# Block-causal attention with a SwiGLU layer: the seven products of the last 1,024 tokens in two PSUM tiles of one bank, where they stood in one tile of two banks

## The chip, the core and the metric

The kernel runs on one core of one Trainium2 chip. The metric is device time in microseconds (us) of one execution; of several executions the median is given. The core has a matmul engine (TensorE, PE in the profile, with PEld for its weight loads), VectorE (DVE), ScalarE (ACT), GpSimd (POOL) and SyncE (SP), which here mostly issues DMAs. Each engine runs its own instructions in program order; between engines they wait on semaphores.

## The reference, cut to what matters

```python
def _attn_ref(q, k, v):                       # each [8, 8, 576, 64]: batch, head, token, channel
    scores = (1.0 / np.sqrt(64)) * np.matmul(q, k.transpose(0, 1, 3, 2))
    scores = np.where(mask, scores, -1e9)     # a query sees the blocks of 64 tokens up to its own
    attn = softmax(scores)
    return np.matmul(attn, v)

x = attn_out.transpose(0, 2, 1, 3).reshape(4608, 512)
g, val = x @ w_gate, x @ w_val                # 512 x 1536 each
return (g * sigmoid(g) * val) @ w_out         # 1536 x 512
```

All is 32-bit floating point. The kernel keeps every operand as a high and a low part and computes a product as three matmuls: high x high, high x low, low x high.

## The kernel before, in words

**Tasks and planner.** `tile_block_causal_attention_swiglu_kernel` runs nothing at first. It records tasks with `add` (line 154): an engine, a cost, a rank, a function that emits the instructions, the tasks it follows, and the buffers (`Buf`, line 134) that it uses. A DMA is recorded by `dma` (line 182) as a task of SP, with `moves`, the time that its bytes take. When all tasks stand, the planner `in_order` (line 1637) plays them through with its own costs (`act_us`, `dve_us`, `mm_us`): on each engine it takes the task of lowest rank whose predecessors are done and whose buffers have a free place, and of a DMA it takes its data to be there at `queue + 0.9`. What it returns is the order in which all is emitted, so its costs set the order of the instructions on each engine and no time on the chip. `keep_busy` (line 1732) puts small filler matmuls (L1741) into gaps that the planner sees on TensorE. The waits between engines come from the tile framework as the instructions are emitted: an instruction that reads or writes a tile waits for those before it that wrote or read the same tile.

**PSUM.** Three pools (lines 310 to 312) fill the eight banks: `at`, two places of two banks ([128, 2, 512] floats); `gv`, two places of one bank; `po`, one place of two banks. The attention uses `at`.

**The first 3,584 tokens** go in 14 tiles of XT = 256 tokens through `feed_forward`. A step makes two chunks of 128 of the 1,536 hidden channels: gate products (L1114 to L1116) into one `gv`, value products into the other, then tanh on ScalarE (L1147) and on VectorE L1150 (which reads the gate's `gv` and frees it) and L1155 (which reads the value's), the split in a high part (L1160, ScalarE) and a low part (L1163, VectorE), and output products (L1205 to L1207) that add up in `po`. `leave` (line 1225) copies finished sums out of PSUM (L1235) and stores them.

**The last 1,024 tokens** go in two pairs (PAIRS = 2) of 512 tokens. `bring_pair` (line 1293) loads the attention's result (L1326, `x_d`) and the inverse sums (`r_load`, L1335, four DMAs from `r_d`), multiplies the two (`divide`, L1341, 1.2 us on VectorE), makes sums of its parts (L1345 to L1347) and splits them into high and low parts (L1361, L1364). This work stands between the steps of the tiles before it. `feed_pair` (line 1373) then makes 12 steps per pair (NFC = 12), each for 128 hidden channels of the gate and of the value layer. It uses a scheme of seven products for a 2 x 2 block product (Strassen's, in Winograd's form), where the sums of weights come from `sum_d` by a load of 2 x 512 KB per step (L1396) and the weights of the output layer from `wo_d` (L1528, 512 KB). In the text the seven products are four groups of matmuls of 256 columns, all on line L1424:

- **P1** (task `u1`): A11 x B11 and A12 x B21, 12 matmuls, into bank 1 of an `at` tile
- **P2** (`u2`): S3 x T3 and S1 x T1, 12 matmuls, into bank 0 of the same tile
- **P3** (`u3`): S2 x T2, 6 matmuls, added to the first half of bank 1
- **P4** (`u4`): A22 x T4 and S4 x B22, 12 matmuls, added to bank 0

Between them the banks are read: ScalarE copies half of P1's bank to SBUF (L1463, task `a1`) and VectorE adds the other half (L1472, `d1`). The same is done for P2's (L1466 `a2`, L1475 `d2`) and, behind P3, L1469 (`a3`) and L1478 (`d3`, no PSUM). L1482 (`d4`) reads the whole of bank 0 behind P4. P3 writes over what `a1` read, so it follows `d1`; P4 follows `d2`. Then come tanh (L1502), the two multiplies (L1505, L1510) and the split (L1515 on ScalarE, L1518 on VectorE) that gives the operand of the **output products** (L1546 to L1548): 12 matmuls of 512 columns per step. They run two steps later: a step's own go to `chain["late"]`, then to `chain["down"]`, and hang on the `u2` of the step after next. They add up over the 12 steps of a pair in four accumulators, two `gv` tiles and the two banks of `po`. Two `at` tiles take turns from step to step.

```python
        accs = [Buf("gv") for _ in range(2)]
        accs += [Buf("po")] * 2
...
            ps, c, t, hh = Buf("at"), Buf("mx", "c"), Buf("t"), Buf("hhl")
...
            u3 = work([product("S2", T2, 1, 0, False, True)], [u2, d1], u2)
            u4 = work([product("A22", T4, 0, 1, False, True), product("S4", B22, 0, 0, False, True)], [u3, d2], u3)
```

Of the kernel before, what the change touches and what calls it, by code (L numbers as in the profile page):

```python
# [12 lines left out]
ALU = mybir.AluOpType  # L13
# [5 lines left out]
def kernel(  # L19
# [17 lines left out]
    nc = tc.nc  # L37
# [10 lines left out]
    NFC = DFF // P  # L48
    SCALE = 1.0 / (D**0.5)
    XT = 256  # L50
# [93 lines left out]
    class Task:  # L144
        def __init__(self, engine, cost, rank, fn, after, bufs, port, mode):
            self.engine, self.cost, self.rank, self.fn = engine, cost, rank, fn
            self.bufs, self.waits, self.next, self.ready = bufs, 0, [], 0.0
            self.moves, self.port, self.mode = 0.0, port, mode

            self.prev = None  # L150

# [17 lines left out]
    def act_us(n, psum=False, more=0.0):  # L169
        return (0.05 if psum else 0.093) + n * 0.000833 + more  # L170
# [1122 lines left out]
    def bring_pair(n, t0):  # L1293
# [26 lines left out]
        for j in range(K):  # L1320
# [30 lines left out]
            l = dma(R, 5e5, load, [*l, turn], [xs], 2, packet=2048)  # L1351
            m = dma(R, 5e5, r_load, [*inv, turn], [rs], 4, packet=2048)
            if n and not j:
                held.extend((n, x) for x in (l, m))
# [18 lines left out]
    def feed_pair(n, t0, xs):  # L1373
# [5 lines left out]
        last_pair = n == PAIRS - 1  # L1379
        accs = [Buf("gv") for _ in range(2)]  # L1380
        accs += [Buf("po")] * 2

        def sums(m):
            return accs[m][0] if m < 2 else accs[m][0][:, m - 2]

# [3 lines left out]
        for i in range(NFC):  # L1389
# [17 lines left out]
            soon, chain["soon"] = chain["soon"], chain["up"]  # L1407
            ps, c, t, hh = Buf("at"), Buf("mx", "c"), Buf("t"), Buf("hhl")

# [7 lines left out]
            def product(a, o, bank, half, begin, end):  # L1417
                def emit(ps=ps, stationary=stationary):
                    to = ps[0][:, bank, half * XT : (half + 1) * XT]
                    for j in range(K):  # L1420
# [13 lines left out]

            def work(products, after, prev):
                def emit(products=products):
# [16 lines left out]

            B11, B21, B22, T1, T2, T3, T4 = range(7)
            u1 = work(
                [product("A11", B11, 1, 0, True, False), product("A12", B21, 1, 1, False, True)],
                [sl, chain["up"]],
                None,
            )
            u2 = work([product("S3", T3, 0, 1, True, False), product("S1", T1, 0, 0, False, False)], [u1], u1)  # L1460

            def copies(c=c, ps=ps):
                nc.scalar.copy(c[0][:, 0], ps[0][:, 1, 0:XT])  # L1463

            def copies3(c=c, ps=ps):
                nc.scalar.copy(c[0][:, 3], ps[0][:, 0, XT : 2 * XT])  # L1466

            def copy_u(t=t, ps=ps):
                nc.scalar.copy(t[0][:, 0:XT], ps[0][:, 1, 0:XT])  # L1469

            def c11(c=c, ps=ps):
                nc.vector.tensor_tensor(c[0][:, 0], ps[0][:, 1, XT : 2 * XT], c[0][:, 0], ALU.add)  # L1472

            def v57(c=c, ps=ps):
                nc.vector.tensor_tensor(c[0][:, 3], ps[0][:, 0, 0:XT], c[0][:, 3], ALU.add)  # L1475
# [4 lines left out]
            def c12(c=c, t=t, ps=ps):  # L1480
                u = t[0][:, 0:XT].rearrange("p (a n) -> p a n", a=1).to_broadcast([P, 2, XT])
                nc.vector.tensor_tensor(  # L1482
                    c[0][:, 1:3], ps[0][:, 0].rearrange("p (a n) -> p a n", a=2), u, ALU.add
                )

            a1 = add("ACT", act_us(XT, True), E, copies, [u1], [ps, c])
            d1 = add("DVE", dve_us(XT), E, c11, [a1], [ps, c])
            a2 = add("ACT", act_us(XT, True), E, copies3, [u2], [ps, c])
            d2 = add("DVE", dve_us(XT), E, v57, [a2], [ps, c])
            u3 = work([product("S2", T2, 1, 0, False, True)], [u2, d1], u2)  # L1490
            u4 = work([product("A22", T4, 0, 1, False, True), product("S4", B22, 0, 0, False, True)], [u3, d2], u3)
            chain["up"] = u4
            in_place[at] = [u4]
            a3 = add("ACT", act_us(XT, True), E, copy_u, [u3], [ps, t])
            d3 = add("DVE", dve_us(XT), E, c22, [a3, d2], [c, t], True)
            d4 = add("DVE", dve_us(w), E, c12, [a3, u4], [ps, c, t])

            def gate():
                return c[0][:, 0:2].rearrange("p a n -> p (a n)")

# [18 lines left out]

            a = add("ACT", act_us(w), E, tanh, [d1, d3, d4], [c, t])  # L1520
            a = add("DVE", dve_us(w), E, silu2, [a], [c, t], True)
            a = add("DVE", dve_us(w), E, gated, [a], [c, t], True)
            a = add("ACT", act_us(w), E, high, [a], [t, hh])
            a = add("DVE", dve_us(w), E, low, [a], [t, hh], True)

# [10 lines left out]
            for x in chain["down"]:  # L1536
                u2.next.append(x)
                x.waits += 1
# [98 lines left out]
    def in_order():  # L1637
# [42 lines left out]
        while events:  # L1680
# [3 lines left out]
            for e in engines:  # L1684
# [28 lines left out]
                if t.moves:  # L1713
                    queue = max(queue, end + 0.65) + t.moves
                    done = queue + 0.9
                heapq.heappush(events, done)
# [64 lines left out]
```

## Time and profile before

| | |
|---|---|
| runs | 1208.89, 1207.72, 1207.88 us: median 1207.88 |
| the profiled execution's own time | 1205.76 us |
| its span in the profile | 1203.7 us (about 2 us of the time lie outside) |
| mean granted clock of TensorE | 0.993 of full speed |
| busy: PE, DVE, ACT, POOL | 96%, 74%, 55%, 27% of the span |
| the chain that ended last, by engine | PE 81%, DMA 6%, ACT 6%, DVE 5%, SP's queue and issue 1% each |
| DMA | 222.60 MB, 185 GB/s over the span |

Busy time is the time in which an engine has an instruction under way. For TensorE the ends of matmuls are modelled, so distances from start to start are the surer reading: 12 matmuls of a group that follow each other show it. The "idle before" of a row is the time in which the engine had nothing under way ahead of that instruction, and the name behind it is the instruction whose semaphore came last. The granted clock is TensorE's share of full speed (2.4 GHz); 0.50 is the lower of its two levels (1.2 GHz).

### The profile page before, as it was taken

The page shows a single profiled execution, that of the slowest core. Times are in us where ns is not written, and L with a number is a line of the kernel's source. Part 1 is how long each engine was busy: PE and PEld are TensorE (multiplying, and loading weights), DVE is VectorE, ACT ScalarE, POOL GpSimd, SP SyncE. Part 2 cuts the span into 40 slices and gives each one's busy share as a digit, 9 for nine tenths or more (in the row PEclk, how much of TensorE's full clock was granted, in tenths as well). Part 3 has the DMA queues.
Part 4 walks back from the last instruction along what each step waited for, and adds up shares of the span by engine and source line. Part 5 has one row for each costly group of instructions (what it writes and reads, how often), then busy time and mean ns, then how long its engine had stood idle before and what let it go on. Part 6 is the DMA issues. An engine that isn't in the chain of part 4 may idle for free.

```text
span 1203.7 us, 22411 instructions
## 1 busy us (share of the span) xinstructions
PE 1158.4 (96%) x8560; PEld 1032.3 (86%) x8560; DVE 890.5 (74%) x1506; ACT 662.3 (55%) x1222; POOL 326.2 (27%) x139
## 2 busy tenths in 40 slices
PE   8999999999999999999999999999999899889897
PEld 6678778888899989899989989998989888878886
DVE  6989988676788889897988988898974525544443
ACT  6888866637565756654647457577552313322222
POOL 3122100144543253343233334344353000000000
PEclk9999999999999999999999999999999999999999
DMA  8658756766566566766666757665653748555550
GB/s 221 183 147 222 209 175 234 193 184 167 156 163 214 146 191 182 220 180 189 192 192 196 200 164 207 189 198 151 181 163 127 236 148 285 197 201 193 188 180 35
DMA packets 281066, 222.60 MB, mean 185 GB/s; under 512 B 196032, under 2 KB 228048, under 8 KB 280960
## 3 DMA queue, kind: packets, MB, share of 16 engines
q1 hardware_dynamic: 278384, 220.46, 61.7%
q8 instruction: 67, 1.10, 0.4%
q10 hardware_dynamic: 2576, 0.72, 0.3%
q14 instruction: 39, 0.32, 0.1%
HBM read 184.16 MB, written 36.96 MB: 184 GB/s over the span
## 4 chain that ended last, share of the span: by engine, by line
PE 81%; DMA 6%; ACT 6%; DVE 5%; issue 1%; SPq 1%; POOL 0%; DVEq 0%; ACTq 0%; POOLq 0%
PE gv L1114 12%; PE gv L1116 11%; PE gv L1115 11%; PE at L1424 9%; PE at L792 7%; PE po L1205 6%; PE po L1207 6%; PE po L1206 5%; PE at L579 5%; DMA wo<-in_moe_w_out_dram 2%; DMA wo<-r_d 1%; ACT ob L974 1%; DMA wo<-wo_d 1%; PE gv L1546 1%; PE gv L1548 1%
## 5 line engine op out<-in xcount | busy, mean ns | idle before, releaser
L843 POOL PARTITION_ALL_REDUCE mx<-mx x48 | 179.2, 3780 | 242.2 <-DVE mx L720 173.2
L724 POOL PARTITION_ALL_REDUCE mx<-mx x80 | 144.5, 1855 | 353.9 <-DVE mx L720 147.3
L1114 PE MATMUL gv<-xhl,v_all 128*128 128x256 f32 x672 | 190.1, 283 | 1.1 <-DVE t L1150 1.1
L1116 PE MATMUL gv<-xhl,v_all 128*128 128x256 f32 x672 | 187.1, 278 | 0.0
L1115 PE MATMUL gv<-xhl,v_all 128*128 128x256 f32 x672 | 186.9, 278 | 0.0
L748 DVE TENSOR_TENSOR sc<-sc,mx 128x640 f32<-128x640 f32 (+6 forms) x168 | 125.4, 781 | 10.4 <-POOL mx L724 10.4
L1114 PEld LDWEIGHTS gv<-xhl,v_all 128*128 128x128 f32 x672 | 126.4, 188 | 6.0 <-issue 2.5
L752 ACT ACTIVATE sc<-sc 128x1024 f32<-128x1024 f32 (+3 forms) x104 | 106.0, 1031 | 38.7 <-DVE sc L748 38.0
L1115 PEld LDWEIGHTS gv<-xhl,v_all 128*128 128x128 f32 x672 | 126.6, 188 | 0.7
L1116 PEld LDWEIGHTS gv<-xhl,v_all 128*128 128x128 f32 x672 | 126.3, 188 | 0.1
L1205 PE MATMUL po<-wo,hhl 128*128 128x512 f32 x300 | 119.3, 398 | 0.9 <-DMA wo<-wo_d 0.9
L1207 PE MATMUL po<-wo,hhl 128*128 128x512 f32 x300 | 117.3, 391 | 0.2 <-DVE hhl L1163 0.2
L1206 PE MATMUL po<-wo,hhl 128*128 128x512 f32 x300 | 117.5, 392 | 0.0
L720 DVE TENSOR_TENSOR mx<-mx,sc 128x128 f32<-128x128 f32 (+2 forms) x180 | 103.9, 579 | 2.4 <-ACT sc L484 0.5
L1114 PE MATMUL gv<-xhl,g_even 128*128 128x256 f32 x336 | 97.5, 290 | 3.9 <-DVE t L1150 3.9
L1160 ACT CAST hhl<-t 128x512 fp32r<-128x512 f32 x84 | 52.1, 620 | 79.4 <-DVE t L1155 68.8
L1116 PE MATMUL gv<-xhl,g_even 128*128 128x256 f32 x336 | 95.6, 284 | 0.0
L1115 PE MATMUL gv<-xhl,g_even 128*128 128x256 f32 x336 | 95.6, 284 | 0.0
L1114 PE MATMUL gv<-xhl,g_odd 128*128 128x256 f32 x336 | 95.3, 284 | 0.0
L1163 DVE TENSOR_TENSOR hhl<-t,hhl 128x512 fp32r<-128x512 f32 x84 | 74.2, 884 | 27.2 <-ACT hhl L1160 26.5
L1116 PE MATMUL gv<-xhl,g_odd 128*128 128x256 f32 x336 | 93.8, 279 | 0.0
L1115 PE MATMUL gv<-xhl,g_odd 128*128 128x256 f32 x336 | 93.8, 279 | 0.0
(246 smaller groups left out, 2820.3 us busy)
## 6 DMA issues: line engine op xcount, KB each, us to landing
wo<-wo_d SPq DMA_DIRECT2D x176, 512.0 KB
v_all<-sum_d SPq DMA_DIRECT2D x48, 512.0 KB
sum_d<-wo SPq DMA_DIRECT2D x48, 256.0 KB
v<-in_v_dram SPq DMA_DIRECT2D x64, 128.0 KB
out_dram<-ob SPq DMA_DIRECT2D x32, 256.0 KB
qk<-in_q_dram SPq DMA_DIRECT2D x112, 72.0 KB
qk<-in_k_dram SPq DMA_DIRECT2D x104, 72.0 KB
x_d<-xu SPq DMA_DIRECT2D x24, 288.0 KB
```

What stands on the lines that cost most here:

```text
L720: nc.vector.tensor_tensor(into, prev, of(c), op)
L724: nc.gpsimd.partition_all_reduce(m, m, channels=P, reduce_op=bass_isa.ReduceOp.max)
L748: nc.vector.tensor_tensor(piece(c), scores_of(c), m, ALU.subtract)
L752: nc.scalar.activation(x, x, AF.Exp)
L843: nc.gpsimd.partition_all_reduce(m, m, channels=P, reduce_op=bass_isa.ReduceOp.add)
L1114: nc.tensor.matmul(o, lhsT=hi[:, d], rhs=xhi[:, 0:w], start=first, stop=False)
L1115: nc.tensor.matmul(o, lhsT=hi[:, d], rhs=xlo[:, 0:w], start=False, stop=False)
L1116: nc.tensor.matmul(o, lhsT=lo[:, d], rhs=xhi[:, 0:w], start=False, stop=last)
L1205: nc.tensor.matmul(po, lhsT=hi, rhs=whi, start=i + y == 0, stop=False)
L1206: nc.tensor.matmul(po, lhsT=hi, rhs=wlo, start=False, stop=False)
L1207: nc.tensor.matmul(po, lhsT=lo, rhs=whi, start=False, stop=i + y == NFC - 1)
L1424: nc.tensor.matmul(to, lhsT=s, rhs=m, start=begin and j == 0 and s is hi and m is xhi, stop=j == K - 1 and s is lo, skip_group_check=True,)
```

## The change

In `feed_pair` the `at` tile `ps` becomes two `gv` tiles, `ab` for P1 and P3 and `cd` for P2 and P4; both are taken anew in each step, and there are two `gv` places in all, so each step uses the same two banks. The output sums stand in `po` (the first two) and in one `at` tile (the other two). The functions between get new names and one that nothing called goes. Besides, the planner counts 0.08 to 0.11 us more for the ScalarE and VectorE tasks of `feed_pair` and 3 us more until the inverse sums of a pair are there (`m.more`), and in the last step of the last pair the output products that wait hang on `u4` instead of `u2`. What is computed is the same. Lines behind line 1350 move by +1, those behind the removed function by -2.

```diff
-            self.prev = None
+            self.prev, self.more = None, 0.0
...
             m = dma(R, 5e5, r_load, [*inv, turn], [rs], 4, packet=2048)
+            m.more = 3.0
...
-        accs = [Buf("gv") for _ in range(2)]
-        accs += [Buf("po")] * 2
+        accs = [u for u in (Buf("po"), Buf("at")) for _ in range(2)]
 
         def sums(m):
-            return accs[m][0] if m < 2 else accs[m][0][:, m - 2]
+            return accs[m][0][:, m % 2]
...
-            ps, c, t, hh = Buf("at"), Buf("mx", "c"), Buf("t"), Buf("hhl")
+            ab, cd, c, t, hh = Buf("gv"), Buf("gv"), Buf("mx", "c"), Buf("t"), Buf("hhl")
...
-                def emit(ps=ps, stationary=stationary):
-                    to = ps[0][:, bank, half * XT : (half + 1) * XT]
+                def emit(ps=(cd, ab)[bank], stationary=stationary):
+                    to = ps[0][:, half * XT : (half + 1) * XT]
...
-            def copies(c=c, ps=ps):
-                nc.scalar.copy(c[0][:, 0], ps[0][:, 1, 0:XT])
...
+            def copy_1(c=c, ab=ab):
+                nc.scalar.copy(c[0][:, 0], ab[0][:, 0:XT])
...
-            a1 = add("ACT", act_us(XT, True), E, copies, [u1], [ps, c])
-            d1 = add("DVE", dve_us(XT), E, c11, [a1], [ps, c])
-            a2 = add("ACT", act_us(XT, True), E, copies3, [u2], [ps, c])
-            d2 = add("DVE", dve_us(XT), E, v57, [a2], [ps, c])
-            u3 = work([product("S2", T2, 1, 0, False, True)], [u2, d1], u2)
-            u4 = work([product("A22", T4, 0, 1, False, True), product("S4", B22, 0, 0, False, True)], [u3, d2], u3)
+            a1 = add("ACT", 0.11 + act_us(XT, True), E, copy_1, [u1], [ab, c])
+            d1 = add("DVE", 0.08 + dve_us(XT), E, c11, [a1], [ab, c])
+            a2 = add("ACT", 0.11 + act_us(XT, True), E, copy_7, [u2], [cd, c])
+            d2 = add("DVE", 0.08 + dve_us(XT), E, add_5, [a2], [cd, c])
+            u3 = work(ab, [product("S2", T2, 1, 0, False, True)], [u2, d1], u2)
+            u4 = work(cd, [product("A22", T4, 0, 1, False, True), product("S4", B22, 0, 0, False, True)], [u3, d2], u3)
...
-            a3 = add("ACT", act_us(XT, True), E, copy_u, [u3], [ps, t])
-            d3 = add("DVE", dve_us(XT), E, c22, [a3, d2], [c, t], True)
-            d4 = add("DVE", dve_us(w), E, c12, [a3, u4], [ps, c, t])
+            a3 = add("ACT", 0.11 + act_us(XT, True), E, copy_16, [u3], [ab, t])
+            d3 = add("DVE", 0.08 + dve_us(XT), E, c22, [a3, d2], [c, t], True)
+            d4 = add("DVE", 0.08 + dve_us(w), E, c12, [a3, u4], [cd, c, t])
...
             for x in chain["down"]:
-                u2.next.append(x)
+                (u4 if last_pair and i == NFC - 1 else u2).next.append(x)
                 x.waits += 1
...
                 if t.moves:
                     queue = max(queue, end + 0.65) + t.moves
-                    done = queue + 0.9
+                    done = queue + 0.9 + t.more
```

The engines' orders are the same up to about 940 us; behind that they differ, because the planner's costs and buffers do. Three places show how.

First piece: ScalarE in one step of the last 1,024 tokens before, with what each instruction waits for (`PE_49` is a count of TensorE's, `DVE_49` of VectorE's, `Activation_49` of ScalarE's own).

```order
L1463 COPY mx_0_10285<-at_0_185 128x256 [waits PE_49]
L1466 COPY mx_0_10285<-at_0_185 128x256 [waits DVE_49,PE_49]
L1515 CAST hhl_0_115<-t_0_117 128x512 [waits DVE_49]
L1469 COPY t_0_953<-at_0_185 128x256 [waits DVE_49]
L1502 ACTIVATE t_0_953<-mx_0_10285 128x512 [waits DVE_49,Activation_49]
```

and the same step now:

```order
L1464 COPY mx_0_10285<-gv_0_174 128x256 [waits PE_49]
L1467 COPY mx_0_10285<-gv_0_155 128x256 [waits PE_49]
L1513 CAST hhl_0_115<-t_0_117 128x512 [waits DVE_49]
L1470 COPY t_0_953<-gv_0_174 128x256 [waits PE_49]
L1500 ACTIVATE t_0_953<-mx_0_10285 128x512 [waits DVE_49,Activation_49]
```

The instructions stand as they did; the copies of P1 and P3 read one tile (`gv_0_174`), that of P2 the other (`gv_0_155`), and the copy of P2 no longer waits for VectorE.

Second piece: VectorE in the steps of `feed_forward` in which the first pair's inputs are brought, near 940 to 960 us, before (`t` and `gv` are a step's, `wo` holds the loaded inputs, L1364 writes low parts).

```order
L1155 SCALAR_TENSOR_TENSOR t_0_953<-t_0_953,gv_0_155 128x512
L1341 TENSOR_TENSOR wo_0_9562<-wo_0_9562,wo_0_9827 128x1024
L1163 TENSOR_TENSOR hhl_1_114<-t_0_953,hhl_0_113 128x512
L1364 TENSOR_TENSOR parts_0_9876<-wo_0_9562,parts_0_9876 128x256
...
L1150 SCALAR_TENSOR_TENSOR t_0_117<-t_0_117,gv_0_174 128x512
L1155 SCALAR_TENSOR_TENSOR t_0_117<-t_0_117,gv_0_155 128x512
L1163 TENSOR_TENSOR hhl_1_116<-t_0_117,hhl_0_115 128x512
L1341 TENSOR_TENSOR wo_0_9919<-wo_0_9919,wo_0_9562 128x1024
L1345 TENSOR_TENSOR wo_0_9987<-wo_0_9919 128x2x256
```

and now:

```order
L1155 SCALAR_TENSOR_TENSOR t_0_953<-t_0_953,gv_0_155 128x512
L1163 TENSOR_TENSOR hhl_1_114<-t_0_953,hhl_0_113 128x512
L1341 TENSOR_TENSOR wo_0_9562<-wo_0_9562,wo_0_9827 128x1024
...
L1155 SCALAR_TENSOR_TENSOR t_0_117<-t_0_117,gv_0_155 128x512
L1163 TENSOR_TENSOR hhl_1_116<-t_0_117,hhl_0_115 128x512
L1150 SCALAR_TENSOR_TENSOR t_0_953<-t_0_953,gv_0_174 128x512
L1155 SCALAR_TENSOR_TENSOR t_0_953<-t_0_953,gv_0_155 128x512
L1163 TENSOR_TENSOR hhl_1_114<-t_0_953,hhl_0_113 128x512
L1341 TENSOR_TENSOR wo_0_9827<-wo_0_9827,wo_0_9981 128x1024
```

The first L1341 has moved behind the L1163 of its step. The second has moved by a whole step: behind the next L1150, L1155 and L1163.

Third piece: TensorE in one step of the second pair now (`sc`, `v` hold the operands, `v_all` the sums of weights). The L1424 rows ahead of the output products are the end of P2, those behind them P3.

```order
L1424 MATMUL gv_0_155<-sc_0_10483,v_all_73 128x256 x2
L1424 MATMUL gv_0_155<-sc_0_10483,v_all_74 128x256
L1544 MATMUL po_0_238<-wo_0_10109,hhl_0_113 128x512
...
L1546 MATMUL at_0_229<-wo_0_10109,hhl_1_114 128x512
L1424 MATMUL gv_0_174<-sc_0_10483,v_all_73 128x256 x2
L1424 MATMUL gv_0_174<-sc_0_10483,v_all_74 128x256
```

The 12 output products stand between P2 and P3 here, where before they stood between P3 and P4.

## Rows read from the trace of the kernel before

**Rows 1.** The page: busy time, share of the span and instructions of each engine.

```profile
PE 1158.4 (96%) x8560; PEld 1032.3 (86%) x8560; DVE 890.5 (74%) x1506; ACT 662.3 (55%) x1222; POOL 326.2 (27%) x139
```

**Rows 2.** Waits on PE: us in total, times, the longest in us.

```profile
PE at L1424 <- DVE mx L1472: 18.4, 20, 1.0
PE gv L1114 <- DVE t L1150: 5.1, 2, 3.9
PE at L1424 <- DVE mx L1475: 2.9, 2, 2.5
```

**Rows 3.** Timeline, PE, 1147 to 1157: start, us, instructions [idle before <-what ended it].

```profile
1147.90 1.58 PE L1424 MATMUL at<-sc,g_odd 128*128 128x256 f32 x12
1149.31 1.57 PE L1424 MATMUL at<-sc,v_all 128*128 128x256 f32 x12
1151.81 0.95 PE L1424 MATMUL at<-sc,v_all 128*128 128x256 f32 x6 [0.92 <-DVE mx L1472]
1152.60 0.39 PE L1546 MATMUL gv<-wo,hhl 128*128 128x512 f32 x1
...
1155.34 0.87 PE L1424 MATMUL at<-v,v_all 128*128 128x256 f32 x6
1156.75 1.59 PE L1424 MATMUL at<-sc,g_even 128*128 128x256 f32 x12
```

**Rows 4.** Timeline, ACT and DVE, the same step.

```profile
1150.92 0.37 ACT L1463 COPY mx<-at 128x256 f32<-128x256 f32 x1 [1.40 <-PE at L1424]
1151.33 0.42 DVE L1472 TENSOR_TENSOR mx<-at,mx 128x256 f32<-128x256 f32 x1 [1.08 <-ACT mx L1463]
...
1156.95 0.69 DVE L1482 TENSOR_TENSOR mx<-at,t 128x512 f32<-128x512 f32 x1 [2.20 <-PE at L1424]
```

**Rows 5.** Timeline, PE and DVE, 942 to 967: the steps that the second piece of order shows.

```profile
942.10 0.28 PE L1114 MATMUL gv<-xhl,g_even 128*128 128x256 f32 x1
...
945.35 0.28 PE L1115 MATMUL gv<-xhl,v_all 128*128 128x256 f32 x1
...
955.76 0.28 PE L1116 MATMUL gv<-xhl,v_all 128*128 128x256 f32 x1
959.96 0.58 PE L1114 MATMUL gv<-xhl,g_even 128*128 128x256 f32 x1 [3.92 <-DVE t L1150]
...
966.06 0.29 PE L1115 MATMUL gv<-xhl,v_all 128*128 128x256 f32 x1
...
953.70 1.23 DVE L1341 TENSOR_TENSOR wo<-wo,wo 128x1024 f32<-128x1024 f32 x1 [2.21 <-DMA wo<-r_d]
...
959.22 0.68 DVE L1150 SCALAR_TENSOR_TENSOR t<-t,gv 128x512 f32<-128x512 f32 x1
```

**Rows 6.** Timeline, PE, DVE and SP's queue, 1017 to 1036: the second pair's inputs.

```profile
1027.23 0.39 PE L1548 MATMUL po<-wo,hhl 128*128 128x512 f32 x1
1030.15 1.09 PE L1424 MATMUL at<-xhl,v_all 128*128 128x256 f32 x6 [2.53 <-DVE mx L1475]
...
1035.34 0.87 PE L1424 MATMUL at<-xhl,v_all 128*128 128x256 f32 x6
...
1025.22 1.23 DVE L1341 TENSOR_TENSOR wo<-wo,wo 128x1024 f32<-128x1024 f32 x1 [2.29 <-DMA wo<-wo_d]
...
1017.12 2.46 SPq L1335 DMA_DIRECT2D wo<-r_d  x4
```

**Rows 7.** Timeline, PE, the last output products.

```profile
1194.70 0.39 PE L1548 MATMUL po<-wo,hhl 128*128 128x512 f32 x1
1196.03 0.50 PE L1546 MATMUL gv<-wo,hhl 128*128 128x512 f32 x1 [0.94 <-ACT hhl L1515]
...
1197.09 0.40 PE L1546 MATMUL gv<-wo,hhl 128*128 128x512 f32 x1
```

**Rows 8.** Windows: stretch, us, busy PE, PEld, DVE, ACT, POOL, PE clock, DMA share, GB/s.

```profile
960.00:965.80 5.80, 5.80 (x27) 5.80 (x28) 1.38 (x2) 0.87 (x2) 0.00 (x0) 0.50 0.87 346
1060.00:1070.00 10.00, 9.08 (x66) 8.39 (x66) 4.25 (x9) 2.87 (x6) 0.00 (x0) 1.00 0.55 162
```

More of the change, by code (lines that the diff above doesn't have):

```diff
@@ L1433, in product, with work @@
                 return emit, o
-            def work(products, after, prev):
+            def work(ps, products, after, prev):
                 def emit(products=products):
@@ L1455, in feed_pair @@
             u1 = work(
+                ab,
                 [product("A11", B11, 1, 0, True, False), product("A12", B21, 1, 1, False, True)],
@@ L1459, in feed_pair @@
             )
-            u2 = work([product("S3", T3, 0, 1, True, False), product("S1", T1, 0, 0, False, False)], [u1], u1)
-            def copies(c=c, ps=ps):
-                nc.scalar.copy(c[0][:, 0], ps[0][:, 1, 0:XT])
[L1465 to L1472, printed above, removed]
@@ L1474, in v57, with copy_7, copy_16 @@
-            def v57(c=c, ps=ps):
-                nc.vector.tensor_tensor(c[0][:, 3], ps[0][:, 0, 0:XT], c[0][:, 3], ALU.add)
+            u2 = work(cd, [product("S3", T3, 0, 1, True, False), product("S1", T1, 0, 0, False, False)], [u1], u1)
+            def copy_1(c=c, ab=ab):
+                nc.scalar.copy(c[0][:, 0], ab[0][:, 0:XT])
+            def copy_7(c=c, cd=cd):
+                nc.scalar.copy(c[0][:, 3], cd[0][:, XT : 2 * XT])
+            def copy_16(t=t, ab=ab):
+                nc.scalar.copy(t[0][:, 0:XT], ab[0][:, 0:XT])
@@ L1477, in c22, with c11, add_5, c12 @@
+            def c11(c=c, ab=ab):
+                nc.vector.tensor_tensor(c[0][:, 0], ab[0][:, XT : 2 * XT], c[0][:, 0], ALU.add)
+            def add_5(c=c, cd=cd):
+                nc.vector.tensor_tensor(c[0][:, 3], cd[0][:, 0:XT], c[0][:, 3], ALU.add)
             def c22(c=c, t=t):
                 nc.vector.tensor_tensor(c[0][:, 3], c[0][:, 3], t[0][:, 0:XT], ALU.add)
-            def c12(c=c, t=t, ps=ps):
+            def c12(c=c, t=t, cd=cd):
                 u = t[0][:, 0:XT].rearrange("p (a n) -> p a n", a=1).to_broadcast([P, 2, XT])
@@ L1482, in c12 @@
                 nc.vector.tensor_tensor(
-                    c[0][:, 1:3], ps[0][:, 0].rearrange("p (a n) -> p a n", a=2), u, ALU.add
+                    c[0][:, 1:3], cd[0].rearrange("p (a n) -> p a n", a=2), u, ALU.add
                 )
-            a1 = add("ACT", act_us(XT, True), E, copies, [u1], [ps, c])
-            d1 = add("DVE", dve_us(XT), E, c11, [a1], [ps, c])
-            a2 = add("ACT", act_us(XT, True), E, copies3, [u2], [ps, c])
-            d2 = add("DVE", dve_us(XT), E, v57, [a2], [ps, c])
@@ L1492, in feed_pair @@
+            u4 = work(cd, [product("A22", T4, 0, 1, False, True), product("S4", B22, 0, 0, False, True)], [u3, d2], u3)
             chain["up"] = u4
             in_place[at] = [u4]
-            a3 = add("ACT", act_us(XT, True), E, copy_u, [u3], [ps, t])
-            d3 = add("DVE", dve_us(XT), E, c22, [a3, d2], [c, t], True)
-            d4 = add("DVE", dve_us(w), E, c12, [a3, u4], [ps, c, t])
-            def gate():
-                return c[0][:, 0:2].rearrange("p a n -> p (a n)")
+            a3 = add("ACT", 0.11 + act_us(XT, True), E, copy_16, [u3], [ab, t])
@@ L1518, in low @@
                 nc.vector.tensor_tensor(hh[1], t[0], hh[0].bitcast(F32), ALU.subtract)
[L1520 to L1524, printed above, removed]
+            a = add("ACT", 0.11 + act_us(w), E, tanh, [d1, d3, d4], [c, t])
+            a = add("DVE", 0.08 + dve_us(w), E, silu2, [a], [c, t], True)
+            a = add("DVE", 0.08 + dve_us(w), E, gated, [a], [c, t], True)
+            a = add("ACT", 0.1 + act_us(w), E, high, [a], [t, hh])
+            a = add("DVE", 0.08 + dve_us(w), E, low, [a], [t, hh], True)
             wo = Buf("wo", "out")
```

## The prediction

> **What bounds the kernel now.** I read the page first: TensorE is busy for 96% of the span [rows 1], so only what makes TensorE stand still, or run at its lower clock, can cost or give time. Next the list of waits on TensorE [rows 2]: its longest entry is a wait of the seven products (L1424) for the VectorE add L1472, 20 times, 18.4 us together. Two more belong to the same stretch or its start: 5.1 us (2 times, the longest 3.9) of gate products behind the VectorE instruction L1150, and 2.9 us (2 times) behind the add L1475. Then the timeline of one step in the last 1,024 tokens [rows 3, 4], and the three places where that stretch stumbles otherwise [rows 5 to 7].
>
> In one step [rows 3] P1 starts at 1147.90 and P2 at 1149.31, so 12 matmuls of 256 columns take 1.41 us. P2 should end at 1150.72, but P3 starts only at 1151.81: 1.09 us lost. P3's six take 0.79 us up to 1152.60 instead of half of 1.41, 0.08 more: the refill after a stop. The wait costs **1.17 us**, against 0.92 us of idle time in the row. A step lasts 8.85 us (1147.90 to 1156.75); without the wait it would last 7.68. The reason stands in [rows 4]: P1 is complete at 1149.31, yet the copy L1463 that reads it starts at 1150.92, after an idle time of 1.40 us that TensorE ends, that is, after P2, which writes the other bank of the same tile. Then come the copy (0.37) and the add L1472 at 1151.33 (0.42), and 0.06 us later P3 may start. Nothing of P3 needs P2.
>
> **The change part by part.** *Two tiles instead of one.* The copy L1463 waits for P1 alone. It can start 0.31 us after P1's last matmul has started, which is how long the add L1482 takes to follow P4 ([rows 3, 4]: P4's last six start at 1155.34 + 0.71 = 1156.05, the last at 1156.64, L1482 at 1156.95). From there 0.37 + 0.04 + 0.42 + 0.06: P3 is free 1.2 us after P1's last matmul has started, while P2 alone runs 1.41 us. In the built order the output products stand behind P2 in most steps and give 2.74 us more (1152.60 to 1155.34). So the 20 waits go: 20 x 1.17 = **-23.4 us**.
>
> What is late next? The two tiles are now written again in every step, where two pairs of banks alternated before. P1 of the next step waits for the copy L1469 behind P3: P4 (1.41) covers it, and it needs 0.31 + 0.37 + 0.06 after P3's last start, so 0.8 us remain. P2 of the next step waits for the add L1482 behind P4 (0.69 us): free 0.31 + 0.69 + 0.06 = 1.06 us after P4's last start, wanted 0.12 + 1.41 = 1.53 us after it; 0.47 us remain. That is the narrowest place, and VectorE stood idle for 2.20 us before that add [rows 4], so nothing queues ahead of it. I take nothing for both. ScalarE and VectorE do the same instructions as before. The added 0.08 to 0.11 in the planner's costs only change its order.
>
> *VectorE's order before the last 1,024 tokens.* The planner now counts 3 us more for the loads of the inverse sums (the four r_d transfers). It puts the multiply L1341, which waits for them, behind other work (second piece of order). Before, the second L1341 stood ahead of the L1150 of a step whose gate products were done. It started at 953.70, when its transfers had landed, and L1150 came at 959.22; TensorE's last matmul had started at 955.76, the next at 959.96 [rows 5]. At the usual 0.11 us spacing that is 4.1 us. The granted clock was then 0.50, the lower of its two levels (1.2 GHz), from 960 to 965.8, against 1.00 (2.4 GHz) in a later stretch [rows 8]. From 959.96 to 966.06 stand 28 spacings; the same 28 took 3.25 us from 942.10 to 945.35 [rows 5]: 2.85 us more. In the new order L1150 comes in its own step, and L1341 one step later, when its transfers, issued some 2.5 us later, have landed long since. Moving four r_d loads behind one weight load on SP's queue costs nothing as long as they land within that step (8 us). **-6.9 us**.
>
> *The same for the second pair's inputs.* One step waited 2.53 us for L1475, itself behind an L1341 that started at 1025.22, 5.6 us after its last load was issued (1017.12 + 2.46) [rows 6]. From the last matmul before it (1027.23, due to be followed at 1027.46) to 1030.15 are 2.7 us; then 30 matmuls took 5.19 us (to 1035.34) where 30 x 0.1175 = 3.53: 1.66 us. The other wait of this kind is 2.9 - 2.53 = 0.37, with the refill 0.6. Together -5.0 us, if the new order loses nothing there. It does lose something: these loads now wait for the buffer of an output product and, laid out from the rows above, land at about the time the add behind P4 is due. That add then comes some 1.0 us late behind L1341 to L1347. With refills I put 1.5 us for this and 0.2 for a step before it: **-3.3 us** net.
>
> *First steps, last step.* In the first two steps and the last one nothing stands between P3 and P4. P4 waits for the copy and add of P2, 1.2 us after P2's last start, and P3 covers 0.82 of that: 0.37 + 0.08 = 0.45 each, three times, and 0.3 for P3 of the third step behind the copies of the tile before: **+1.6 us**. At the end, the output products of the last three steps now run behind the last P4, 36 in a row. Before, the last twelve began at 1196.03 where 1194.70 + 0.23 was possible, and their first three took 1.06 us (to 1197.09) instead of 0.69 [rows 7]: 1.1 + 0.37. Now 24 matmuls (5.5 us) cover the chain from P4 to the last operand, which took 4.0 us there: **-1.4 us**. The output sums in po and at instead of gv and po are copied by the same four copies; at the change of pair the first two run beside the second half of the output products, so I count nothing. One added filler matmul of 64 columns: nothing.
>
> *Sum.* -23.4 - 6.9 - 3.3 + 1.6 - 1.4 = -33.4 us on the profiled execution's 1205.76, that is 1172.4. The median of the runs lies 2.1 above that execution, so the forecast is **1174.5 us**.
>
> *A rule that speaks against it.* In the trace, four banks in turn did not keep TensorE from waiting in each step [rows 3]. The Trainium skill, "Perfetto Trace Analysis", section Matmul Optimizations, asks that all 8 PSUM banks be used, and its section Optimizing Tensor Performance that independent groups rotate through different banks, so that one is emptied while the next is written. The change gives up two banks of that rotation in the last 1,024 tokens, and by the rule the steps should get longer; that is the second rival below. The trace agrees with the reason, but shows that a tile, not a bank, is what the copy waited on.
>
> **The rivals.** *Late loads.* The r_d loads for the second pair come later than I lay out, and VectorE holds up the add that P2 waits for, by 2 us or more, with the lower clock after it. For: it happened at 1030.15, at 2.7 + 1.66 = 4.4 us, and a step shorter by 1.17 us leaves less room. Against: the planner counts 3 us more. Two such places: up to +8.7, so up to 1183. Also covered by this: a weight load that is late by up to 2 us in the last steps of the tile before.
>
> *Emptying is exposed (slower).* With two banks instead of four, P1 and P2 of each step wait for the copy and the add of the step before. Priced as the old wait, 1.17 each: 24 x 2.34 = 56.2 instead of 23.4 now, +32.8, less the 6.9: 1233.8. It decides from about 1.4 us of new waiting per step (33.4 / 24) beyond the old wait's removal. For: no second pair of banks. Against: margins of 0.8 and 0.47 us, and idle times of 1.40 and 2.20 us on ScalarE and VectorE just ahead [rows 4].
>
> *The copies still wait for both.* If a wait on TensorE's count still covers P2, only the order and the end gain: 1207.9 - 6.9 - 1.4 = 1199.6. Against: in the new order the copy of P2 has lost its wait on VectorE, as it must if the tiles are apart.
>
> *Transfers become the bound.* Two loads of 512 KB of sums and one of weights per step, 1.57 MB, in 7.68 us are 205 GB/s; the windows show 162 at a DMA share of 0.55, and 346 at 0.87 [rows 8]. So there is room; if not, steps stay near 8.85 and the time near 1199.
>
> **How the numbers follow.** Forecast 0.76, late loads 0.14, copies still waiting 0.03, transfers 0.03, exposed emptying 0.04. The range takes the first two: 1170 (nothing lost in the second pair's loads, and the runs' own scatter) to 1186 (two late loads, a weight load late by 2 us). Only the exposed emptying ends above 1207.88, and a mild form of it could meet it; a measurement of this kernel tells 0.2%, 2.4 us. Faster 0.95, same 0.01, slower 0.04.
>
> **What would show it.** Right: no wait of L1424 for the add behind P1 in the list; steps of 7.7 us; the copy of P1 starting during P2; no gap near 956 and no clock of 0.50 after it; at the end one run of 36 output products. Wrong: a new entry of L1424 behind L1483 (the former L1482) or L1470 (L1469) in many steps, steps of 8.8 us, or DMA share near 1 in the last 200 us.

## The result, and the profile after

| | before | changed |
|---|---|---|
| median of 4 runs | 1207.8 us (1207.34 to 1208.89) | 1173.26 us (1170.72 to 1179.16) |
| profiled execution | 1205.76 us, span 1203.7 | 1172.47 us, span 1170.7 |
| mean granted clock | 0.993 | 0.998 |

The ratio is 0.972, with a 95% interval of 0.9682 to 0.9757. The forecast was 1174.5 (1170 to 1186), so sign and size came out, and each term of the sum came out within 0.8 us. The reason given for the largest term is one of two, as the experiments show: the two tiles remove the waits by themselves, but so does the new order of the output products, and the change brings both.

The page of the changed kernel's profile, against [rows 1]:

```profile
PE 1146.6 (98%) x8562; PEld 1025.3 (88%) x8562; DVE 891.4 (76%) x1506; ACT 663.1 (57%) x1222; POOL 327.6 (28%) x139
```

VectorE and ScalarE do what they did (890.5 and 662.3 us before). TensorE is busy for 11.8 us less; the stretch at the lower clock [rows 8] and the slow starts behind stops are gone, and how the 11.8 us divide between them was not measured. The rest of the gain, 21 us of span, is idle time.

The list of waits on TensorE in the changed kernel, the entries of the seven products, the gate products and the added fillers (us in total, times, the longest), against [rows 2]:

```profile
PE gv L1424 <- DVE mx L1476: 0.7, 3, 0.2
...
PE gv L1114 <- DVE t L1150: 0.3, 1, 0.3
...
PE gv L1739 <- DVE mx L1483: 0.2, 1, 0.2
```

The entry of 20 times and 18.4 us is gone, and so is the 3.9 us behind L1150.

One step of the last 1,024 tokens in the changed kernel, timeline of PE, ACT and DVE (start us, us, instructions, idle before), against [rows 3, 4]:

```profile
1045.22 1.58 PE L1424 MATMUL gv<-parts,g_odd 128*128 128x256 f32 x12
1046.63 0.87 PE L1424 MATMUL gv<-xhl,v_all 128*128 128x256 f32 x6
...
1048.04 0.40 PE L1544 MATMUL po<-wo,hhl 128*128 128x512 f32 x1
...
1050.77 0.87 PE L1424 MATMUL gv<-xhl,v_all 128*128 128x256 f32 x6
...
1052.89 1.59 PE L1424 MATMUL gv<-parts,g_even 128*128 128x256 f32 x12
1054.32 0.84 PE L1424 MATMUL gv<-xhl,v_all 128*128 128x256 f32 x6
...
1046.83 0.38 ACT L1464 COPY mx<-gv 128x256 f32<-128x256 f32 x1
...
1053.09 0.69 DVE L1483 TENSOR_TENSOR mx<-gv,t 128x512 f32<-128x512 f32 x1 [0.58 <-PE gv L1424]
```

P1 starts at 1045.22, P2 at 1046.63, the output products at 1048.04, P3 at 1050.77 and the next P1 at 1052.89: 7.67 us, with no idle time in a PE row. From the fourth step to the last but one, 19 of the 20 steps have their output products between P2 and P3 like this. The copy of P1 (L1464) starts at 1046.83, while P2 runs. The narrowest place is where it was put: L1483 ends its work at 1053.09 + 0.69 = 1053.78, and P2 of the next step is due at 1054.32; less the 0.06 us until TensorE may start, 0.48 us remain (forecast 0.47).

### The profile page after: what moved, and what is told of

Its sections match the earlier page's. It is cut to its first block, busy times and chain, and to the rows that moved or that the text cites. A ratio compares the mean times of both kernels' runs of the same rounds, so it can differ in the third digit from the quotient of the medians.

```text
span 1170.7 us, 22454 instructions
## 1 busy us (share of the span) xinstructions
PE 1146.6 (98%) x8562; PEld 1025.3 (88%) x8562; DVE 891.4 (76%) x1506; ACT 663.1 (57%) x1222; POOL 327.6 (28%) x139
## 5 line engine op out<-in xcount | busy, mean ns | idle before, releaser
L1114 PE MATMUL gv<-xhl,g_odd 128*128 128x256 f32 x336 | 94.6, 282 | 0.0
L1147 ACT ACTIVATE t<-gv 128x512 f32<-128x512 f32 x84 | 50.2, 598 | 77.6 <-PE gv L1116 77.4
L1163 DVE TENSOR_TENSOR hhl<-t,hhl 128x512 fp32r<-128x512 f32 x84 | 75.2, 895 | 24.5 <-ACT hhl L1160 24.0
L1116 PE MATMUL gv<-xhl,g_odd 128*128 128x256 f32 x336 | 93.1, 277 | 0.0
```

The lines of the kernel that those rows point to most:

```text
L1114: nc.tensor.matmul(o, lhsT=hi[:, d], rhs=xhi[:, 0:w], start=first, stop=False)
L1116: nc.tensor.matmul(o, lhsT=lo[:, d], rhs=xhi[:, 0:w], start=False, stop=last)
```

## The experiments

P3 must not start before the copy and the add of P1 are done. Three theories say what keeps TensorE from waiting for them. **A:** either of two things is enough alone: the copy freed from P2 by the two tiles, or the 12 output products between P2 and P3, which give the copy and the add time. The change brings both, the second through the planner's costs. **B:** only the two tiles do it. **C:** only the order does it. A step with the output products between P2 and P3 is called covered below. Each ratio is against the kernel before, run again beside it; its medians there were 1206.73, 1206.69 and 1204.16 us, not 1207.8.

### One tile, all the rest of the change

The kernel before, with these lines besides `m.more`:

```diff
-            a1 = add("ACT", act_us(XT, True), E, copies, [u1], [ps, c])
+            a1 = add("ACT", 0.11 + act_us(XT, True), E, copies, [u1], [ps, c])
...
-                u2.next.append(x)
+                (u4 if last_pair and i == NFC - 1 else u2).next.append(x)
```

(and the same 0.08 to 0.11 on the other ScalarE and VectorE tasks).

> The kernel before (one tile of two banks per step, two such tiles in turn, output sums where they were) with all the rest of the change: the planner's costs, the 3 us more for the inverse sums, the last step's output products behind P4. In its built order the 12 output products stand between P2 and P3 in 21 of 24 steps, as in the changed kernel. Theory A (either one suffices: the copy of P1 freed from P2, or 2.74 us of output products ahead of P3, which cover the 1.2 us of copy and add): no wait in those 21 steps, 1.17 us only in the three steps without output products there; about 1174.5 + 1.2, so 1174 to 1178. Theory B (the two tiles are what removes the waits): steps of 8.85 us stay and the time is 1207.8 - 6.9 - 4 - 1.4 = 1195 to 1199.

Measured: 1181.86 us (1179.47 to 1183.78), ratio 0.9802 (0.9753 to 0.9851). That is nearer to A, but outside its range. The 15 steps from the ninth to the last but one take 7.65 to 7.67 us with one tile, as the changed kernel's do. Four steps are not covered (the first three and the last), and not three, and the first two of them lose far more than 1.17 us, as the timelines of ACT and PE in the first step show:

```profile
977.34 0.37 ACT L1464 COPY mx<-at 128x256 f32<-128x256 f32 x1 [2.40 <-PE at L1425]
...
978.22 0.97 PE L1425 MATMUL at<-xhl,v_all 128*128 128x256 f32 x6 [0.92 <-DVE mx L1473]
980.51 1.37 PE L1425 MATMUL at<-sr,v_all 128*128 128x256 f32 x6 [1.33 <-ACT t L1470]
```

P3 waits 0.92 us as before, and then P4 waits 1.33 us more for L1470, the copy of P3's result. P4 writes bank 0 and L1470 reads bank 1; with one tile it waits all the same. The first three steps take 12.03, 10.51 and 8.82 us (8.13, 8.20 and 7.86 in the changed kernel), the first at a mean granted clock of 0.86, and the last one 1.9 us longer. So the two tiles are worth 8.6 us between the medians here. In the profiles, from the first P1 to the end, they are worth 9.8 us: 7.2 in the first three steps, 1.9 in the last and 0.8 around the loads of the second pair.

### Two tiles, the old costs

The changed kernel with `0.11 +`, `0.1 +` and `0.08 +` taken out of all `add` calls of `feed_pair`.

> The changed kernel without the 0.08 to 0.11 us that the planner counts more for ScalarE and VectorE in the last 1,024 tokens. Two tiles stay, but in 20 of 24 steps the output products stand between P3 and P4, as before the change. Theory A: P3 is free 1.2 us after P1's last start, P2 runs 1.41, so no wait in these steps: within 2 us of the changed kernel, 1171 to 1176. Theory C (only the place of the output products matters): the wait of 1.17 us returns in about 20 steps: 1194 to 1199. In between, about 0.3 us per step (1178 to 1181), would mean that something on ScalarE stands ahead of the copy of P1.

Measured: 1171.74 us (1171.42 to 1175.31), ratio 0.9728 (0.9687 to 0.9769): as the changed kernel. P3 follows P2 directly in 22 of the 24 steps, and no wait for L1473 is in the list. C falls. The 15 steps from the ninth to the last but one take 7.73 us on average instead of 7.66. One step, from the timelines of PE, ACT and DVE:

```profile
1060.44 0.87 PE L1424 MATMUL gv<-xhl,v_all 128*128 128x256 f32 x6
...
1061.85 0.87 PE L1424 MATMUL gv<-xhl,v_all 128*128 128x256 f32 x6
...
1060.64 0.37 ACT L1464 COPY mx<-gv 128x256 f32<-128x256 f32 x1
...
1060.67 0.69 DVE L1503 SCALAR_TENSOR_TENSOR t<-t,mx 128x512 f32<-128x512 f32 x1 [0.76 <-ACT t L1500]
1061.28 0.42 DVE L1473 TENSOR_TENSOR mx<-gv,mx 128x256 f32<-128x256 f32 x1
```

P2 starts at 1060.44 and P3 at 1061.85. The copy of P1 comes when the prediction says, 0.32 us after P1's last matmul has started. The add L1473 comes 0.23 us later than the prediction says (1061.28 instead of 1060.64 + 0.37 + 0.04 = 1061.05), because the multiply L1503 stands ahead of it on VectorE. It is done at 1061.70, so with the 0.06 us of [rows 3, 4] P3 could start at 1061.76: 0.09 us to spare, and 0.06 to 0.09 in all but one of the steps behind the seventh. So the two tiles are enough alone, but narrowly.

### The two tiles alone

The changed kernel without `m.more = 3.0`, without the added costs and with `u2` in the last step.

> The kernel before with the two tiles and the moved output sums alone: planner's costs, loads and the last step as before. VectorE's L1341 stands where it stood, so the 6.9 us near 956 and the 4 to 5 us at the second pair's inputs stay. Theory A: 1207.8 - 23.9 + 1.2 = 1185, range 1182 to 1188. If the two tiles did everything: 1174. If they did nothing alone: 1204 to 1208.

Measured: 1184.45 us (1181.58 to 1188.74), ratio 0.9829 (0.9784 to 0.9875), as A has it. From the seventh on the steps take 7.7 us. What stays lost is where the prediction put it, in VectorE's order, but not in the sizes that it gave. In the profiled execution the stretch near 956 loses 2.8 us and not 6.9 (33.1 us from the gate product of [rows 5] to the first P1, where 30.3 are left without a loss), and the fourth to the sixth step, at the second pair's inputs, lose 8.4 us and not 4 to 5. That the sum came out is in part luck. From this kernel's timelines of DVE and PE, near the second pair's inputs:

```profile
1019.34 1.23 DVE L1341 TENSOR_TENSOR wo<-wo,wo 128x1024 f32<-128x1024 f32 x1 [3.69 <-DMA wo<-wo_d]
1020.48 0.68 DVE L1482 TENSOR_TENSOR mx<-gv,t 128x512 f32<-128x512 f32 x1
1021.09 0.68 DVE L1345 TENSOR_TENSOR wo<-wo 128x512 f32<-128x512 f32 x1
...
1021.22 0.97 PE L1423 MATMUL gv<-xhl,v_all 128*128 128x256 f32 x6 [3.61 <-DVE mx L1482]
```

VectorE stands 3.69 us in front of L1341 until a load is in, and the add that P2 of the next step waits for stands behind it: 3.61 us of TensorE, in a step of 13.14 us. TensorE then runs at a granted clock of 0.50 from 1022.2 to 1025.6.

### The 3 us for the inverse sums alone

```diff
+            m.more = 3.0
...
-                    done = queue + 0.9
+                    done = queue + 0.9 + t.more
```

> The kernel before with the 3 us more for the inverse sums alone (one tile, old costs). VectorE's L1341 moves behind the next step's work near 956 and near 1020. If the step at 956 was lost to L1341 as the prediction says: 1207.8 - 6.9 - 3 to 5, and the waits behind P2 mostly stay (17 to 20 of them): 1194 to 1199. If the 6.9 us were lost to something else (the clock or a late load): 1206 to 1208, with a stop of several us in the same steps.

Measured: 1200.9 us (1197.27 to 1205.32), ratio 0.995 (0.9925 to 0.9976). The list of waits:

```profile
PE at L1425 <- DVE mx L1473: 20.3, 22, 1.0
PE at L1425 <- ACT t L1470: 2.7, 2, 1.3
```

The stop near 956 is gone, as is the low clock [rows 5, 8]; the window of that stretch (us, busy PE, PEld, DVE, ACT, POOL, PE clock, DMA share, GB/s):

```profile
940.00:975.00 35.00, 35.00 (x259) 33.03 (x258) 19.40 (x36) 9.77 (x23) 0.00 (x0) 1.00 0.72 235
```

From the gate product of [rows 5] to the first P1 are 30.3 us, as in the changed kernel. The steps of the last 1,024 tokens still take 8.86 us, now 22 of them with the wait, and the first two are as dear as in the first experiment (12.00 and 10.52 us); that is why it ends above its range.

### The changed kernel again, and two small terms

> The changed kernel once more, unedited, beside the three below: how far its runs scatter. If the 1179 among its first runs is a late load of the second pair's inputs with the lower clock after it, single runs of some 4 to 8 us more come again at a mean clock of 0.996 or less; if it was the first part of the kernel, the clock stays at 0.998. Median 1171 to 1176.

Measured: 1173.07 us (1172.19 to 1174.9), ratio 0.9722 (0.9693 to 0.9752); no run far off the others came. From the first P1 to the end of the span are 196.5 us in both profiles of this kernel (974.17 to 1170.7, 976.65 to 1173.1). What differs lies ahead of the last 1,024 tokens. What the single 1179.16 was stays open.

The next kernel has `u2.next.append(x)` in the last step again:

> The changed kernel with the last step's waiting output products on u2 again, so 12 of them stand between P2 and P3 of the last step and 24 at the end. The prediction's -1.4 for the end and +0.45 for the last step's P4: the wait of 0.9 us behind L1513 comes back and the P4 wait of 0.2 goes; net 0.9 us longer. From the end of the last P4 on (without 12 products at 0.228) 11.5 us instead of 10.0. If the order at the end does not matter: no wait and the same span.

Measured: 1175.02 us (1172.24 to 1182.43), ratio 0.9742 (0.9707 to 0.9778): runs scatter too much for 0.9 us, but the stretch from the first P1 to the end (973.37 to 1170.8) is 197.4 us, 0.9 more, and the wait is back:

```profile
1163.10 0.50 PE L1544 MATMUL po<-wo,hhl 128*128 128x512 f32 x1 [0.88 <-ACT hhl L1513]
```

The next has `m.more = 5.0`:

> The changed kernel with 5 us instead of 3 for the inverse sums. VectorE's second L1341 then stands behind L1483 of its step and not ahead of it, and the tile's last output products stand between P3 and P4 or P2 and P3 in the first two steps. If the 0.79 us of the step near 1021 come from L1341 to L1347 standing ahead of L1483, and the 0.47 and 0.54 us of the first two steps from nothing covering P4's wait: both go, 1.7 to 2 us less than the changed kernel (all 24 steps at 7.65 to 7.75). If they come from the loads themselves: the same time.

Measured: 1173.69 us (1170.19 to 1177.21), ratio 0.9725 (0.9693 to 0.9757). All steps but the last take 7.63 to 7.67 us, and the stretch from the first P1 to the end (975.06 to 1169.5) is 194.4 us, 2.1 less. L1341 stands behind L1483 now, in this kernel's timeline of DVE:

```profile
1021.21 0.69 DVE L1483 TENSOR_TENSOR mx<-gv,t 128x512 f32<-128x512 f32 x1 [0.58 <-PE gv L1424]
1021.82 1.22 DVE L1341 TENSOR_TENSOR wo<-wo,wo 128x1024 f32<-128x1024 f32 x1
```

So the 0.79 us of that step and the 1.0 us of the first two were the order's doing.

### How narrow the emptying is

L1483 issued three times in the changed kernel:

```diff
-                nc.vector.tensor_tensor(
-                    c[0][:, 1:3], cd[0].rearrange("p (a n) -> p a n", a=2), u, ALU.add
-                )
+                for _ in range(3):
+                    nc.vector.tensor_tensor(
+                        c[0][:, 1:3], cd[0].rearrange("p (a n) -> p a n", a=2), u, ALU.add
+                    )
```

> The changed kernel with L1483 (the add that empties P2's and P4's tile) issued three times with the same operands and result, so that the tile comes free some 1.2 us later (two more at 0.60). The prediction's margin there is 0.47 us per step: P2 of the next step should wait 0.7 to 0.8 us with its refill, 23 times, 16 to 19 us: 1189 to 1193. If the margin is larger than the prediction says (1.2 or more), nothing changes; if the tiles' emptying were already on the path, it would be 23 x 1.2 = 28 us: 1201.

Measured: 1200.03 us (1196.44 to 1202.06), ratio 0.9934 (0.991 to 0.9958): more than forecast, as the two added instructions take 0.725 us each and not 0.60, and the refill costs 0.17. The time is the one given for an emptying that was on the path already (1201), so it can't tell the two readings apart; the starts in the timelines can. From this kernel's timelines:

```profile
1101.66 2.14 DVE L1484 TENSOR_TENSOR mx<-gv,t 128x512 f32<-128x512 f32 x3 [0.31 <-PE gv L1424]
...
1101.46 1.59 PE L1424 MATMUL gv<-sc,g_even 128*128 128x256 f32 x12
1103.86 1.68 PE L1424 MATMUL gv<-sc,v_all 128*128 128x256 f32 x12 [0.81 <-DVE mx L1484]
```

The tile comes free 2.14 - 0.69 = 1.45 us later. P2 starts 2.40 us after P1 instead of 1.43: 0.97 later. The margin was 1.45 - 0.97 = 0.48 us, the prediction's 0.47; without a margin P2 would start 1.45 us later. A step takes 8.80 us, 1.14 more: 0.97 and the refill.

### The same threefold add with one tile, two in turn

The first experiment's kernel with the same three lines.

> The first experiment's kernel (one tile, two in turn, the rest of the change) with the add behind P4 (L1483) issued three times, which with the two tiles cost 0.98 us per step ahead of P2 and the refill. Here the next step writes the other pair of banks. If that wait came from the reuse of the same two banks in every step, it is gone and the time is the first experiment's 1181.9 plus at most 3: 1180 to 1185. If VectorE's 1.45 us more per step were the cause by itself: 1181.9 + 26 = 1208.

Measured: 1195.85 us (1193.64 to 1196.79), ratio 0.9918 (0.9889 to 0.9947): both readings were wrong. The list of waits:

```profile
PE at L1425 <- DVE mx L1476: 6.8, 14, 2.2
PE at L1425 <- DVE mx L1473: 4.8, 4, 1.9
```

The wait for the threefold add is gone, as four banks in turn should have it. Another comes in its place: P3 waits for L1476, the add of P2 in the other bank of its tile, which the longer chain on VectorE has delayed past the output products. From the eighth on a step takes 8.08 us, 0.42 over 7.66. Four banks in turn give back 0.72 of the 1.14 us, and the wait for the other bank of the shared tile costs 0.42.

### Planner's numbers alone

The kernel before with the added costs of the first experiment and `m.more = 5.0`; tiles, sums and the last step as before.

> The kernel before with nothing but planner's numbers changed: the 0.08 to 0.11 us more for ScalarE and VectorE, and 5 us more for the inverse sums. One tile of two banks per step, two in turn, sums where they were. In its built order output products stand between P2 and P3 in every step but the first. Theory A (either one suffices): all steps but the first at 7.66 us, the first 1.2 us longer, the wait of 0.9 us at the end stays: the time of the run with 5 us (1173.7) plus 1.2 + 0.4, so 1173 to 1178. If the two tiles are still worth something in covered steps: above 1180.

Measured: 1173.88 us (1173.36 to 1175.52), ratio 0.9744 (0.9716 to 0.9771), against 0.972 for the changed kernel. It has 5 us where the change has 3; with 3 us and one tile the first experiment took 1181.86. It has one tile of two banks, and of the 20 waits one is left, in the first step, beside the one at the end:

```profile
PE gv L1547 <- ACT hhl L1516: 1.6, 1, 1.6
...
PE at L1425 <- DVE mx L1473: 0.9, 1, 0.9
```

A step in the middle, from its timelines of PE and ACT:

```profile
1092.06 1.57 PE L1425 MATMUL at<-sc,v_all 128*128 128x256 f32 x12
1093.47 0.40 PE L1547 MATMUL gv<-wo,hhl 128*128 128x512 f32 x1
...
1096.20 0.87 PE L1425 MATMUL at<-sc,v_all 128*128 128x256 f32 x6
...
1093.67 0.37 ACT L1464 COPY mx<-at 128x256 f32<-128x256 f32 x1 [0.67 <-PE at L1425]
```

The copy of P1 still waits for the end of P2 (1093.67, after idle time that TensorE ends), and it does not matter: output products run from 1093.47 to 1096.20. B falls. Against the two tiles with the same 5 us it takes 2.9 us more from the first P1 to the end (197.3 and 194.4): 1.2 in the first step, the rest in the last one and behind it, where it also keeps `u2`.

### The costs alone

The kernel before with the added costs and nothing else.

> The kernel before with the 0.08 to 0.11 us more alone. The output products stand between P2 and P3 from the second step on, VectorE's L1341 stands where it stood before. Theory A: 1206.7 - 20 x 1.19 + 1.2 = 1184, and the losses near 956 and at the second pair's inputs remain, as with the two tiles alone (1184.45): 1180 to 1188. Theory B (the tiles are needed): 1204 to 1208.

Measured: 1184.31 us (1183.34 to 1185.6), ratio 0.9826 (0.9798 to 0.9854): the same as the two tiles alone (0.9829), as A has it. All steps but the first and those at the second pair's inputs take 7.66 us. The stretch near 956 loses 5.1 us in its profile (35.4 and not 30.3 us to the first P1).

### Two small terms together

The kernel with 5 us, and in the last pair the output products of its third-last step (the tenth; its index is NFC - 3) in two halves:

```diff
-            for x in chain["down"]:
-                (u4 if last_pair and i == NFC - 1 else u2).next.append(x)
+            for k, x in enumerate(chain["down"]):
+                (u4 if last_pair and i == NFC - 1 and k else u2).next.append(x)
```

> The changed kernel with 5 us instead of 3 and with the output products of step 10 of the last pair in two halves, of which 6 stand between P2 and P3 of the last step and 6 behind P4. The wait of 0.2 us of the last P4 with its refill (0.48 together) should go, and 18 output products (4.1 us) still cover the last operand: 0.3 to 0.5 us less than with 5 us alone from the first P1 to the end. If 18 don't cover it, a wait behind L1513 of up to 0.5 us comes.

Measured: 1170.23 us (1169.27 to 1171.11), ratio 0.9708 (0.9681 to 0.9736). The stretch from the first P1 to the end (973.29 to 1167.3) is 194.0 us, 0.4 less than with 5 us alone, and neither the seven products nor the output products of these tokens are in the list of waits any more. It is 2.5 us faster than the changed kernel in that stretch (196.5); the intervals of the ratios overlap.

## Why the prediction was right, and where it was not

The terms, from the profiled executions. The stretch that the change leaves alone took 1.8 us more in the changed kernel's execution (the same gate product starts at 942.10 before and 943.87 now), so differences are taken from there.

| term of the sum | forecast | measured |
|---|---|---|
| 20 waits for the add behind P1 | -23.4 | -24.0 (20 steps of 177.2 us together, less 20 x 7.66) |
| VectorE's order near 956 | -6.9 | -7.0 (to the first P1: 37.31, now 30.30) |
| second pair's inputs | -3.3 | -4.1 (4.94 us over 7.66 before, 0.87 now) |
| first steps and last step | +1.6 | +1.7 (0.47, 0.54, 0.20 and 0.49) |
| the end | -1.4 | -1.5 (11.5 from the last P4 on, now 12.77 - 2.73) |
| sum | -33.4 | -34.9 |

With the 1.8 us of the untouched part that makes -33.1; the profiled executions differ by 33.3.

The losses before are read from the execution that the forecast was worked out from, so the table tests what is left of them now. How large they are from one execution to the next is another matter. Near 956, VectorE's order in the two tiles alone and in the costs alone is that of before, and in their profiles it costs 2.8 and 5.1 us where it costs 7.0 here, with L1341 waiting for the `r_d` loads each time and the granted clock at 0.50 for no time, 3.4 us and 6.8 us. That the 3 us more remove this loss is shown, by the run with these alone; that -6.9 is its size is true of one execution, and that the medians agree with it so closely is in part luck. The prediction also holds that a measurement of this kernel tells 2.4 us; later runs of the kernel before lie 12.7 us apart.

**Right.** The wait was priced at 1.17 us from distances between starts, refill included, and measured 1.20. That the two tiles remove it is shown by the runs with two tiles and the old costs. The margin of 0.47 us came out at 0.48 and was confirmed by the threefold add. The loads of the second pair did what was laid out: in the changed kernel the add behind P4 stood behind L1341 to L1347, and the step took 0.79 us more, where 1.5 were reckoned. The late-loads rival, 2 us or more, did not come in either profile of the changed kernel.

**Wrong: what the largest term was credited to.** The step "Two tiles instead of one" ends with "So the 20 waits go", and the sentence ahead of it names the output products behind P2 only as something on top. "The added 0.08 to 0.11 in the planner's costs only change its order" put that order at nothing. The room that the working left, 0.12 + 1.41 - 1.2 = 0.33 us, was 0.06 to 0.09 us in the kernel with two tiles and the old costs, because L1503 is missing in the working; with 2.74 us of output products in between this did not matter. The runs show four cases of a step:

| | output products behind P3 | output products behind P2 |
|---|---|---|
| one tile | 8.86 us (before) | 7.66 us (planner's numbers alone) |
| two tiles | 7.73 us (two tiles, old costs) | 7.66 us (changed) |

Either one removes the wait, and the second then adds next to nothing. For the same reason the rival "the copies still wait for both" was priced wrong: it gave 1199.6, and the kernel in which they do wait, with all the rest of the change, takes 1181.86. The trace of before had the answer. Only 20 of its 24 steps wait; in the other four the output products stand behind P2. One of them, from the timelines of PE and ACT of the kernel before:

```profile
1014.24 1.60 PE L1424 MATMUL at<-parts,g_even 128*128 128x256 f32 x12
...
1017.03 0.40 PE L1546 MATMUL gv<-wo,hhl 128*128 128x512 f32 x1
1019.78 0.87 PE L1424 MATMUL at<-xhl,v_all 128*128 128x256 f32 x6
...
1021.90 1.34 PE L1424 MATMUL at<-parts,g_odd 128*128 128x256 f32 x10
...
1017.33 0.35 ACT L1463 COPY mx<-at 128x256 f32<-128x256 f32 x1
```

The copy comes after P2 there as well, at 1017.33 (there the tanh L1502 stands ahead of it on ScalarE as well), and the step takes 1021.90 - 1014.24 = 7.66 us. The last PE row is cut off by the end of the window. A count of 20 and not 24 was read in [rows 2] and not asked about. A slip without effect: P1's row in [rows 3] ends at 1147.90 + 1.58 = 1149.48, and not at 1149.31.

**The rule on banks.** With two banks in use instead of four the steps did not get longer, because the emptying had 0.48 us to spare; when it took 1.45 us more, two banks cost 1.14 us per step and four in turn 0.42, which the list of waits puts down to the shared tile. The Trainium skill, "Perfetto Trace Analysis", section Optimizing Tensor Performance, asks that independent groups rotate through different banks; in these runs more banks in the rotation save time only where a bank is not yet empty when it is wanted.

## What to carry to other kernels

When a change brings a new structure and a new order together, try each alone: here the planner's numbers alone, with 5 us for the change's 3, gave nearly the whole gain (0.9744 against 0.972), and with the 3 us and the changed last step some 70% of it (0.9802). Before pricing a wait that most steps show, look at the steps that don't show it; they tell what hides it. And a large tile makes an instruction wait for readers of a part that it does not touch, so where nothing else runs in between, one tile per bank is worth having: 9.8 us here, nearly all of it in four steps that were not covered. A loss that hangs on when a load lands has no fixed size: read it in more than one profile before it goes into a sum.

## What had not been expected

- With one tile, P4 in bank 0 waited 1.33 us for a copy out of bank 1, besides P3's 0.92, and TensorE then ran at its lower clock for a while: a step of 12.03 us, mean clock 0.86.
- Three adds that write the same place take 2.14 us, 0.725 us for each further one. In the two tiles alone L1345, which writes elsewhere, starts 0.61 us behind the same add (1020.48 and 1021.09). That the shared place is the reason was not tested.
- Runs of the kernel before scatter from 1201.04 to 1213.73 us, at mean clocks from 0.99 to 1.00, far more than the four shown at first. Two profiles of the changed kernel agree to 0.1 us in its last 196.5 us, so differences of 1 to 2 us are read from that stretch and not from medians.
